# Attention and two feed-forward layers on one core: the softmax's output transposed by VectorE after a trip to DRAM

## The chip, the cores and the metric

The kernel runs on one core of one Trainium2 chip. The metric is the device time of one execution in microseconds (us).

## The reference

Three stages follow each other, all in fp32:

```python
# window attention: q, k, v are (4, 8, 576, 64)
scores = scale * np.matmul(q, k.transpose(0, 1, 3, 2))
mask = (rel >= 0) & (rel < 64)                 # rel = query position - key position
attn = np.exp(scores - max) ; attn = attn / (sum + 1e-09)
x = np.matmul(attn, v)                         # -> 2304 tokens x 512
# layer 1: w_in 512 x 2048, w_out 2048 x 512
h = x @ w_in ; r = np.maximum(h, 0.0) ; x = (r * r) @ w_out
# layer 2: the same sizes, with a rational function P(h) / Q(h) in place of r * r
return (g @ w_out).astype(np.float32)
```

## The kernel before

**Tiling.** The 2304 tokens are 18 sub-blocks of 128 (numbered 0 to 17) and five blocks: 0 to 3 of 512 tokens (four sub-blocks each), 4 of 256 (sub-blocks 16 and 17). A sub-block has two groups of 64 queries (`gl`); each sees 128 keys. Layer 1 goes through the blocks, and while block b runs, the attention of block b+1 is computed in between. So the attention of sub-blocks 8 to 11 lies in block 1, that of 12 to 15 in block 2, and that of 16 and 17 in block 3. Layer 2 follows.

**A step of a layer** is one of 16 pieces of the hidden dimension: 12 matmuls of 128x512 into `h` (L619; three products each stand for one fp32 product, split into a high and a low part), `mid1` (ScalarE takes relu and squares, VectorE subtracts for the low part, L692), and, one step later, 12 matmuls into `acc` (L638). A block of layer 1 ends with `evac1`: the result is split into `xh` and `xl` and stored to DRAM (`x2h_d`, `x2l_d`, 1 MB each).

**The attention of a sub-block** is cut into slots: `slot_q` and `slot_k` bring q and k into the layout with the head dimension on partitions; `slot_s` multiplies them (scores, L525); `softmax` masks (VectorE, L542), takes the exponential (ScalarE, L547) and multiplies by the reciprocal sum (VectorE, L551, L552 and L555); two `slot_p`, one for each group, transpose the result p, four TensorE transposes of 128x128 each (L568), and evict them from PSUM (L573, ScalarE or VectorE); `slot_x` multiplies with v (L585). From a block's second sub-block on, `slot_sx` puts the product with v of one sub-block right behind the scores of the next.

**Squares.** From sub-block 12 (`NPE`) on, q and k are not transposed by TensorE: a transfer within DRAM (`squares`) puts their 32x32 squares at the places where they belong after a transpose, the load takes them from there, and VectorE transposes within each square (L463, L485).

**Weights of layer 2** are converted during blocks 1 to 3 (`convert`): a load of the raw fp64 words (`raw`), work on ScalarE (L399, L418) and VectorE (L401 to L419), two stores (`w2h_d`, `w2l_d`).

**What sets the order.** A planner (`Plan`) takes each piece of work with a fixed cost per engine, buffers that it reads and writes, and a due time, and lists the pieces in the order in which they would start. Each engine then works in this order. All DMAs are issued by SyncE's queue (SP) in the planner's order too, and a DMA that waits holds back those behind it. To the planner all DMAs are one engine with size/360 ns each and 2 us until the data is there.

```python
KTP, QTP, SM, PT = ring("kT", 2), ring("qT", 2), ring("sm", 2), ring("pT", 2)
plan.add({"pe": 430}, tr, [src], [ps], due)                                  # slot_p
plan.add({"pe": 2150 if x_of else 900}, mm, [qt, kt] + values[0], ps + values[1], due)
```

Of the kernel before, what the change touches and what calls it, by code (L numbers as in the profile page):

```python
# [9 lines left out]
F32 = mybir.dt.float32  # L10
F32R = mybir.dt.float32r
U32 = mybir.dt.uint32
ACTF = mybir.ActivationFunctionType
ALU = mybir.AluOpType
# [122 lines left out]
def dve(n, fast=False, ptr=0):  # L137
    return 68 + 1.042 * n / (2 if fast else 1) + 61 * ptr
# [3 lines left out]
def window_attention__moe_relu2__moe_rational_kernel(  # L142
# [30 lines left out]
    NSUB = NT // 128  # L173
    blocks = [(t0, min(512, NT - t0)) for t0 in range(0, NT, 512)]
    NB = len(blocks)
    orders = (list(range(NB)), list(range(NB - 2)) + [NB - 1, NB - 2])
    NS0 = blocks[0][1] // 128
    NPE = sum(n for _, n in blocks[:3]) // 128
    scale = 1.0 / float(D) ** 0.5

    ctx.enter_context(tc.manual_schedule())
    sb = ctx.enter_context(tc.tile_pool(name="sb", bufs=1))
    dram = ctx.enter_context(tc.tile_pool(name="dram", bufs=1, space=bass.MemoryType.DRAM))
    psum = ctx.enter_context(tc.tile_pool(name="psum", bufs=1, space=bass.MemoryType.PSUM))

    V, A, P, T = nc.vector, nc.scalar, nc.gpsimd, nc.tensor
    plan = Plan()
# [6 lines left out]
    SMALL = [("cb", 2), ("coef", 6), ("na", 4), ("b1", 1)] + [(f"{x}{i}", 4) for x in ("nm", "su", "rs") for i in range(4)]  # L194
    TAGS = ([("ident", [128, 128], F32), ("mask", [128, 2, 128], F32)] +
            [(f"kT{i}", [128, HP, W + 128], F32) for i in range(2)] + [(x, [128, n], F32) for x, n in SMALL] +
            [("pad", [128, 224], F32)] +
            [(f"wi{x}{j}", [128, DM], F32R) for j in range(NF) for x in "hl"] +
            [(f"wo{j}", [128, KT, 2, 2, 128], F32R) for j in range(NF // 2)] +
            [(f"x{x}{i}", [128, 4, KT, 128], F32R) for i in range(2) for x in "hl"] +  # L200
# [10 lines left out]
    mask = sb.tile([128, 2, 128], F32, tag="mask", name="mask")  # L211
# [19 lines left out]

    sq_d = {x: dram.tile([128, HP, (NSUB - NPE) * 4, 32], F32, name=f"{x}_squares_d") for x in "kq"}


    turn = {}

    def buf(place, shape, dtype=F32, pool=sb, view=None):

        if not isinstance(place, str):
            n = turn.get(place, 0)  # L240
            turn[place] = n + 1
            place = place[n % len(place)]

        def make():
            t = pool.tile(shape, dtype, tag=place, name=place)
            return view(t) if view else t

        return Buf(plan, place, make)

    def ring(name, n):  # L250
        return tuple(f"{name}{i}" for i in range(n))
# [3 lines left out]

    ALL_PS = ("t0", "h0", "t1", "h1", "acc0", "acc1", "acc2", "acc3")
    LD, RAW, CV = ring("ld", 6), ring("raw", 3), (0, 1, 2)
    KTP, QTP, SM, PT = ring("kT", 2), ring("qT", 2), ring("sm", 2), ring("pT", 2)
    shared = {}

    def part(place, tag, shape, dtype, view, gen=0):
# [48 lines left out]
    def due_h(l, bi, j):  # L310
        return start[l, bi] + span[l, bi] * j / NF
# [4 lines left out]
    def load(dst, pieces, size, slow=1, reads=(), due=None):  # L316
        def emit(_):
            for o, i in pieces():
                nc.sync.dma_start(out=o, in_=i)
        return plan.add({"dma": size / 360 * slow}, emit, reads, [dst], due)  # L320
# [9 lines left out]
    def nat_buf(x, i):  # L330
        if i < NS0:
            return early(NF - 1 - i, x, D)
        return buf(LD, [128, H, D])
# [3 lines left out]
    def squares(nm, c, last, token):  # L337


        src = {"k": k, "q": q}[nm]  # L340
        pieces = list(toks(NPE * 128, NT - NPE * 128))
        b = sq_b[nm, c, last] = Buf(plan, f"{nm}_squares{c}{last}", None)
# [10 lines left out]
    def load_qk(i):  # L353
        for x, (nm, src) in enumerate((("k", k), ("q", q))):
            t = nat_buf(x, i)
            if i >= NPE:
                b0 = (i - NPE) * 4
                load(t, lambda t=t, nm=nm: [(
# [95 lines left out]
    def ps_buf():  # L454
        return buf(ps_places[0], [128, 512], F32, psum, cols(128))

    qT, kT, sm, pT = {}, {}, {}, {}

    def slot_q(i, due):
        src = nat["q", i]  # L460
        if i >= NPE:
            t = qT[i] = buf(QTP, [128, HP, 128])
# [15 lines left out]
    def slot_k(i, due):  # L478
        src = nat["k", i]
        if i >= NPE:  # L480
            t = kT[i] = buf(KTP, [128, HP, W + 128])
# [52 lines left out]
    def softmax(i, gl, ps):  # L534
        t = early(NF - 5 - i, gl, 128) if i < NS0 else buf(SM, [128, 4, 128])
        sm[i, gl] = t
        kind = int((2 * i + gl) % GPB == 0)
        nm, su, rs = (buf(ring(x, 4), [128, 4]) for x in ("nm", "su", "rs"))

        def top(_):  # L540
            for c in range(4):
                V.tensor_tensor_reduce(out=t.t[:, c, :], in0=ps.t[:, c, :], in1=mask[:, kind, :], scale=-scale,  # L542
                                       scalar=-NEG, op0=ALU.add, op1=ALU.min, accum_out=nm.t[:, c:c + 1])

        def exp(_):
            for c in range(4):
                A.activation(out=t.t[:, c, :], in_=t.t[:, c, :], func=ACTF.Exp, scale=-1.0, bias=nm.t[:, c:c + 1],  # L547
                             accum_out=su.t[:, c:c + 1])

        def norm(_):  # L550
            V.tensor_scalar(out=rs.t, in0=su.t, scalar1=1e-9, scalar2=None, op0=ALU.add)  # L551
            V.reciprocal(out=rs.t, in_=rs.t)  # L552

        def mul(e):
            (P if e == "pool" else V).tensor_tensor(out=t.t, in0=t.t, in1=rs.t.unsqueeze(2).to_broadcast([128, 4, 128]),  # L555
                                                    op=ALU.mult)

        plan.add({"dve": 850}, top, [ps], [t, nm])
        plan.add({"act": 1550}, exp, [nm, t], [t, su])
        plan.add({"dve": 350}, norm, [su], [rs])  # L560
        plan.add({"pool": 1400} if i < NS0 else {"dve": 690}, mul, [rs, t], [t])

    def slot_p(i, n, due):
        src, ps = sm[i, n], ps_buf()

        def tr(_):
            for c in range(4):
                T.transpose(ps.t[:, c, :], src.t[:, c, :], ident)  # L568

        plan.add({"pe": 430}, tr, [src], [ps], due)  # L570
        t = pT[i, n] = early(NF - 5 - i, 2 + n, 128) if i < NS0 else buf(PT, [128, 4, 128])
        plan.add({"act": act(512, True), "dve": dve(512)}, lambda e: (
            A.copy(out=t.t, in_=ps.t) if e == "act" else V.tensor_copy(t.t, ps.t)), [ps], [t])  # L573

    def slot_x(i, due, ps=None):
        joined = ps is not None
        ps = ps or ps_buf()
        vg = [nat["v", 2 * i + gl] for gl in range(2)]
        pt = [pT[i, n] for n in range(2)]

        def mm(_):
            for hp in range(HP):
                for gl in range(2):
                    for e in range(2):
                        T.matmul(  # L585
                            out=ps.t[e * 64:(e + 1) * 64, hp, gl * W:(gl + 1) * W],
                            lhsT=vg[gl].t[:, 2 * hp + e, :],
                            rhs=pt[gl].t[:, hp, (e ^ gl) * 64:((e ^ gl) + 1) * 64],
                            start=True, stop=True,
                        )  # L590

        if joined:
            return vg + pt, [ps], mm
        plan.add({"pe": 1250}, mm, vg + pt, [ps], due)
        split_x(i, ps)
# [208 lines left out]
    for l in range(2):  # L804
# [4 lines left out]
        for s in range(len(steps) + 1):  # L809
            lag = LAGS[l][0] if s < len(steps) - NF else LAGS[l][1]  # L810
            if s < len(steps):
                bi, j = steps[s]
                due = due_h(l, bi, j)
                if l == 0 and j == 0 and bi + 1 < NB:
                    f = blocks[bi + 1][0] // 128
# [12 lines left out]
                hp = h_mm(l, bi, j, due)  # L828
                gs[s] = (mid1 if l == 0 else mid2)(bi, j, hp)
                if l == 0 and NF - 2 <= s < NF - 2 + 4 * HP:  # L830
                    z, c = divmod(s - NF + 2, 2 * HP)
# [11 lines left out]
            if l == 0 and s < len(steps):  # L843
                while slots and slots[0][1] < due_h(0, bi, j + 1):
                    x, d = slots.pop(0)
# [43 lines left out]
```

## Time and profile before

| | us |
|---|---|
| median of 3 runs | 887.34 (884.33 to 888.93) |
| the profiled execution | 890.21 |
| its span, first to last instruction | 888.4 |
| TensorE busy | 870.5 (98%) |
| VectorE busy | 674.3 (76%) |
| ScalarE busy | 561.0 (63%) |
| mean granted TensorE clock | 0.996 |

The span starts with the first instruction; 1.8 us of the execution lie around it. TensorE's matmuls are pipelined and overlap in the records, so the price of one is read from the start of one to the start of the next, not from its length. The granted clock is a share of the full 2.4 GHz; its other level is 0.5. In the rows, PE is TensorE, DVE VectorE, ACT ScalarE, SPq SyncE's queue.

### The profile page before, as it was taken

Reading aid. Unit: us, or ns where it says so; the run is one execution under the profiler, and the core shown is the slowest. Engines: PE = TensorE matmul, PEld = TensorE weight load, DVE = VectorE, ACT = ScalarE, POOL = GpSimd, SP = SyncE. Lnnn points to the kernel's source line nnn. Section 1 sums busy time; section 2 is a strip of 40 time slices with the busy share of each in tenths; the row PEclk is TensorE's granted clock in tenths of the full one; section 3 lists DMA queues with packets and bytes.
Section 4 is the critical chain, followed back from the end, with each engine's and each line's share of the span. In section 5 each row is a group of like instructions: output and inputs, shape, how many; then the busy total and the mean of one; then the engine's idle time right before and its main releaser. Section 6 shows DMA issues by size and latency. Waiting matters only on the chain.

```text
span 888.4 us, 14088 instructions
## 1 busy us (share of the span) xinstructions
PE 870.5 (98%) x5152; PEld 726.5 (82%) x5152; DVE 674.3 (76%) x1435; ACT 561.0 (63%) x1172; POOL 11.5 (1%) x25
## 2 busy tenths in 40 slices
PE   7799999999999999999999999999999999999998
PEld 6678788888878888888899888888888888988886
DVE  6999995666466676754421899999999999999994
ACT  6778774656456554535444766676667667888764
POOL 4000000000000000000000000000000000000000
PEclk9999999999999999999999999999999999999999
DMA  9686662688855453633189910210011002100001
GB/s 230 187 243 199 188 192 84 200 219 220 223 179 184 147 184 141 238 134 126 49 313 372 361 45 0 96 48 1 1 47 48 1 1 94 49 1 24 1 1 48
DMA packets 152998, 113.64 MB, mean 128 GB/s; under 512 B 92769, under 2 KB 131681, under 8 KB 150881
## 3 DMA queue, kind: packets, MB, share of 16 engines
q1 hardware_dynamic: 152928, 112.75, 41.0%
q8 instruction: 40, 0.66, 0.3%
q14 instruction: 30, 0.24, 0.1%
HBM read 81.79 MB, written 34.08 MB: 130 GB/s over the span
## 4 chain that ended last, share of the span: by engine, by line
PE 88%; DVE 6%; DMA 3%; ACT 2%; issue 1%; SPq 0%; POOLq 0%; POOL 0%; ACTq 0%; DVEq 0%
PE h L619 30%; PE acc L640 22%; PE acc L638 19%; PE t L619 11%; PE t L525 1%; DMA raw<-in_moe_w_out_dram 1%; PE t L568 1%; DVE cvr L404 1%; PE h L585 1%; DVE cvr L407 1%; DVE sm L542 1%; DVE g L692 1%; DMA ld<-in_q_dram 0%; PE t L585 0%; DMA raw<-in_moe_w_in_dram 0%
## 5 line engine op out<-in xcount | busy, mean ns | idle before, releaser
L638 PE MATMUL acc<-g,wo 128*128 128x512 f32 (+1 forms) x960 | 215.9, 372 | 0.8 <-DVE g L692 0.8
L638 PEld LDWEIGHTS acc<-g,wo 128*128 128x128 f32 x960 | 167.3, 189 | 31.5 <-DVE g L692 1.4
L619 PE MATMUL h<-xh,wih 128*128 128x512 f32 (+1 forms) x480 | 181.1, 377 | 2.0 <-DVE rs L551 2.0
L619 PE MATMUL h<-xl,wih 128*128 128x512 f32 (+1 forms) x480 | 178.0, 371 | 0.3 <-DVE xl L603 0.3
L619 PE MATMUL h<-xh,wil 128*128 128x512 f32 (+1 forms) x480 | 178.3, 371 | 0.0
L619 PEld LDWEIGHTS h<-xh,wih 128*128 128x128 f32 x480 | 91.0, 190 | 18.0 <-ACT sm L547 2.1
L692 DVE TENSOR_TENSOR g<-cvr,g 128x512 fp32r<-128x512 f32 (+1 forms) x80 | 50.8, 635 | 71.7 <-ACT cvr L690 71.4
L619 PEld LDWEIGHTS h<-xh,wil 128*128 128x128 f32 x480 | 91.1, 190 | 16.0 <-DVE wil L419 0.4
L619 PEld LDWEIGHTS h<-xl,wih 128*128 128x128 f32 x480 | 91.1, 190 | 14.9 <-DVE xl L603 0.6
L685 ACT ACTIVATE cvr<-h 128x512 f32<-128x512 f32 (+1 forms) x80 | 44.3, 554 | 84.9 <-PE h L619 83.0
L640 PE MATMUL acc<-wo,cvr 128*128 128x512 f32 x384 | 93.1, 390 | 0.0
L640 PE MATMUL acc<-wo,g 128*128 128x512 f32 x384 | 93.1, 389 | 0.0
L640 PEld LDWEIGHTS acc<-wo,g 128*128 128x128 f32 x384 | 71.6, 188 | 14.6
L640 PEld LDWEIGHTS acc<-wo,cvr 128*128 128x128 f32 x384 | 71.5, 188 | 14.4
L736 DVE SCALAR_TENSOR_TENSOR kT<-kT,b,sm 128x512 f32<-128x512 f32 (+1 forms) x80 | 55.8, 698 | 16.4 <-ACT kT L731 13.8
L399 ACT ACTIVATE cvr<-raw 128x512 f32<-128x512 f32 x64 | 42.9, 671 | 30.3 <-DMA raw<-in_moe_w_out_dram 13.7
L738 ACT ACTIVATE raw<-kT,cb 128x512 f32<-128x512 f32 (+1 forms) x80 | 54.9, 686 | 8.8 <-DVE kT L736 6.6
L619 PE MATMUL t<-xl,wih 128*128 128x512 f32 (+1 forms) x160 | 58.9, 368 | 0.0
L619 PE MATMUL t<-xh,wil 128*128 128x512 f32 (+1 forms) x160 | 58.8, 368 | 0.0
L619 PE MATMUL t<-xh,wih 128*128 128x512 f32 (+1 forms) x160 | 58.8, 367 | 0.0
L749 DVE SCALAR_TENSOR_TENSOR pT<-pT,coef,raw 128x512 f32<-128x512 f32 (+1 forms) x80 | 55.8, 697 | 1.7
L740 ACT ACTIVATE raw<-raw,cb 128x512 f32<-128x512 f32 (+1 forms) x80 | 54.5, 681 | 1.7
(150 smaller groups left out, 1322.6 us busy)
## 6 DMA issues: line engine op xcount, KB each, us to landing
raw<-in_moe_w_in_dram SPq DMA_DIRECT2D x64, 256.0 KB, 3.4
raw<-in_moe_w_out_dram SPq DMA_DIRECT2D x32, 512.0 KB, 4.5
w2h_d<-raw SPq DMA_DIRECT2D x32, 256.0 KB, 2.1
w2l_d<-cvr SPq DMA_DIRECT2D x32, 256.0 KB, 2.1
ld<-in_v_dram SPq DMA_DIRECT2D x25, 256.0 KB, 3.9
out_dram<-ld SPq DMA_DIRECT2D x18, 256.0 KB, 2.1
x2h_d<-xh SPq DMA_DIRECT2D x4, 1024.0 KB, 5.1
x2l_d<-xl SPq DMA_DIRECT2D x4, 1024.0 KB, 7.7
```

Of the source, the lines that this page charges most:

```text
L399: plan.add({"act": act(DM)}, lambda e: A.activation(out=t.t, in_=raw.t.bitcast(F32)[:, :, 1], func=ACTF.Copy, scale=2.0 ** -112), [raw], [t])
L404: plan.add({"dve": dve(DM)}, lambda e: V.scalar_tensor_tensor(out=u(t), in0=u(t), scalar=3, in1=raw.t[:, :, 1], op0=ALU.logical_shift_left ...
L407: plan.add({"dve": dve(DM)}, lambda e: V.scalar_tensor_tensor(out=u(t), in0=raw.t[:, :, 0], scalar=29, in1=u(t), op0=ALU.logical_shift_rig ...
L619: T.matmul(out=v4(hp.t, n), lhsT=w.t[:, (c ^ 2) * 128:((c ^ 2) + 1) * 128], rhs=x.t[:, :n // 128, c, :], start=(c == 0 and z == 0), stop=( ...
L638: T.matmul(out=v4(acc[l, bi, m].t, n), lhsT=w.t[:, m, :], rhs=y.t[:, :n // 128, :], start=st, stop=en)
L640: T.matmul(out=v4(acc[l, bi, m].t, DM), lhsT=y.t[:, m, :], rhs=w.t, start=st, stop=en)
L685: plan.add({"act": act(n, True)}, lambda e: A.activation(out=r.t[:, :n], in_=hp.t[:, :n], func=ACTF.Relu), [hp], [r])
L692: plan.add({"dve": dve(n)}, lambda e: V.tensor_tensor(out=gl.t[:, :nq], in0=v4(r.t, n), in1=gh.t[:, :nq].bitcast(F32), op=ALU.subtract), [ ...
L736: plan.add({"dve": dve(n, ptr=1)}, lambda e: V.scalar_tensor_tensor(out=f(h2), in0=f(h2), scalar=b1, in1=f(ab), op0=ALU.mult, op1=ALU.add) ...
L738: plan.add({"act": act(n, ptr=1)}, lambda e: A.activation(out=f(y), in_=f(h2), func=ACTF.Ln, scale=2.0 ** -63, bias=cb[:, 0:1]), [h2], [y])
L740: plan.add({"act": act(n, ptr=1)}, lambda e: A.activation(out=f(y), in_=f(y), func=ACTF.Exp, scale=-1.0, bias=cb[:, 1:2]), [y], [y])
L749: plan.add({"dve": dve(n, ptr=1)}, lambda e: V.scalar_tensor_tensor(out=f(u), in0=f(u), scalar=coef[:, 0:1], in1=f(y), op0=ALU.subtract, o ...
```

## The change

From sub-block 8 (`NPD`) on, p takes the way of the squares. The three softmax operations write their tile with the 32-key pieces outermost, then the heads, so that each 32x32 square is complete in itself. After the multiplication the tile is stored to a DRAM tile (256 KB, one DMA), and four DMAs of 64 KB load it into the same tile with the squares rearranged: 32 queries go to 32 partitions' places and the four pieces of keys to the four groups of partitions. `slot_p` is then one VectorE instruction, a transpose within the squares of a 128x512 tile, instead of four TensorE transposes and an eviction. The product with v reads its 64 columns as two runs of 32. The ring `sm` has three tiles instead of two.

```diff
+    NPD = sum(n for _, n in blocks[:2]) // 128
...
+    p_d = dram.tile([NSUB - NPD, 2, 128, 4, 128], F32, name="p_d")
...
-    KTP, QTP, SM, PT = ring("kT", 2), ring("qT", 2), ring("sm", 2), ring("pT", 2)
+    KTP, QTP, SM, PT = ring("kT", 2), ring("qT", 2), ring("sm", 3), ring("pT", 2)
...
+        if i >= NPD:
+            keys = lambda x: x.rearrange("p (k j) -> p k j", j=32)
+            head = lambda c: t.t.rearrange("p k (h j) -> p k h j", j=32)[:, :, c, :]
+            full = lambda: t.t.rearrange("p k (h j) -> p k h j", j=32)
+            sums = lambda: rs.t.unsqueeze(1).unsqueeze(3).to_broadcast([128, 4, 4, 32])
...
-                A.activation(out=t.t[:, c, :], in_=t.t[:, c, :], func=ACTF.Exp, scale=-1.0, bias=nm.t[:, c:c + 1],
+                A.activation(out=head(c), in_=head(c), func=ACTF.Exp, scale=-1.0, bias=nm.t[:, c:c + 1],
...
+        if i >= NPD:
+            d = p_d[i - NPD, gl]
+            b = Buf(plan, f"p_d{i}{gl}", None)
+            load(b, lambda: [(d, t.t)], 1 << 18, reads=[t])
+            load(t, lambda: [(t.t[z * 32:(z + 1) * 32], d[:, z, :].rearrange("(a j) f -> j a f", j=32))
+                             for z in range(4)], 1 << 18, reads=[b])
 
     def slot_p(i, n, due):
-        src, ps = sm[i, n], ps_buf()
+        src = sm[i, n]
+        if i >= NPD:
+            t = pT[i, n] = buf(PT, [128, 4, 128])
+            plan.add({"dve": dve(512)}, lambda e: V.transpose(
+                t.t.rearrange("p a f -> p (a f)"), src.t.rearrange("p a f -> p (a f)")), [src], [t], due)
+            return
+        ps = ps_buf()
...
-                            rhs=pt[gl].t[:, hp, (e ^ gl) * 64:((e ^ gl) + 1) * 64],
+                            rhs=(pt[gl].t[:, (e ^ gl) * 2:(e ^ gl) * 2 + 2, hp * 32:(hp + 1) * 32] if i >= NPD else
+                                 pt[gl].t[:, hp, (e ^ gl) * 64:((e ^ gl) + 1) * 64]),
```

Since the planner lists everything anew, other work moves as well. Two places matter below. The first is SP's queue at the start of block 2, around the stores of block 1's result (`x2h_d`, `x2l_d`). Before:

```order
L319 DMA w2h_d<-raw_2872 128x512
L319 DMA w2l_d<-cvr 128x512
L319 DMA x2h_d<-xh_932 128x2048
L319 DMA x2l_d<-xl_972 128x2048
L319 DMA raw_3076<-in_moe_w_in_dram 128x2x256 x2
```

and with the change, where `sm_2933` and `sm_2944` are the two groups of sub-block 12:

```order
L323 DMA ld_2995<-in_v_dram 128x8x64
L323 DMA p_d<-sm_2933 128x512
L323 DMA ld_3021<-in_v_dram 128x8x64
L323 DMA p_d<-sm_2944 128x512
L323 DMA sm_2933<-p_d 32x4x128 x4
L323 DMA x2h_d<-xh_934 128x2048
L323 DMA sm_2944<-p_d 32x4x128 x4
L323 DMA x2l_d<-xl_974 128x2048
```

The loads of the first group now stand behind the store of the second, and the loads of the second behind the 1 MB store of `xh`. The start of block 1 (sub-block 8) has the same pattern, with the two loads of one raw weight between the second group's store and `x2h_d`. From the store of `xh` of block 0 to that of block 1 SP's list grows from 109 to 149 DMAs.

The second is VectorE at the same place. Before, from the multiplication of sub-block 12's second group on:

```order
L555 TENSOR_TENSOR sm_2953<-sm_2953,rs_3027 128x512
L407 SCALAR_TENSOR_TENSOR cvr<-raw_2909,cvr 128x512
L692 TENSOR_TENSOR g<-cvr,g 128x4x128
L419 TENSOR_TENSOR cvr<-cvr,raw_2909 128x512
L692 TENSOR_TENSOR g<-cvr,g 128x4x128
L401 TENSOR_SCALAR raw_3076<-raw_3076 128x512
```

and with the change (L569 is the multiplication, L718 the subtraction that was L692, L586 the new transpose):

```order
L569 TENSOR_TENSOR sm_2944<-sm_2944,rs_3012 128x512
L717 TENSOR_TENSOR cvr<-cvr 128x512
L733 TENSOR_TENSOR xl_974<-acc_1984,xh_934 128x4x128
L718 TENSOR_TENSOR g<-cvr,g 128x4x128
L405 TENSOR_SCALAR raw_2898<-raw_2898 128x512
L487 COPY kT_3051<-kT_2695 128x4x64
L408 SCALAR_TENSOR_TENSOR cvr<-cvr,raw_2898 128x512
L411 SCALAR_TENSOR_TENSOR cvr<-raw_2898,cvr 128x512
L586 STREAM_TRANSPOSE pT_3066<-sm_2933 128x512
L717 TENSOR_TENSOR cvr<-cvr 128x512
L423 TENSOR_TENSOR cvr<-cvr,raw_2898 128x512
L718 TENSOR_TENSOR g<-cvr,g 128x4x128
```

A transpose that waits for its loads now stands ahead of a subtraction on whose result the matmuls into `acc` wait. On TensorE the slots of p disappear from sub-block 8 on; the products with v of sub-blocks 8 and 12 (each joined to the scores of the next) stand nine and three matmuls later than before, the others at the same place or within a few matmuls.

## Rows read from the trace of the kernel before

**Rows 1.** The chain that ended last, by engine (part 4 of the page).

```profile
PE 88%; DVE 6%; DMA 3%; ACT 2%; issue 1%; SPq 0%; POOLq 0%; POOL 0%; ACTq 0%; DVEq 0%
```

**Rows 2.** By stage: stretch, length, busy of PE, PEld, DVE, ACT, POOL, clock, DMA share, GB/s.

```profile
148.00:245.00 97.00, 96.93 (x640) 79.23 (x639) 58.30 (x147) 54.68 (x126) 0.00 (x0) 1.00 0.80 216
245.00:345.00 100.00, 97.90 (x654) 79.62 (x653) 65.54 (x176) 56.52 (x139) 0.00 (x0) 0.98 0.54 176
345.00:440.00 95.00, 95.00 (x534) 78.03 (x533) 55.22 (x122) 47.01 (x101) 0.00 (x0) 1.00 0.39 136
```

**Rows 3.** Groups by line and shape: busy us, mean ns of one, idle before.

```profile
L568 PE MATMUL t<-ident,sm 128*128 128x128 f32 x112 | 16.8, 272 | 2.1 <-DVE sm L555 2.1
...
L573 ACT COPY pT<-t 128x512 f32<-128x512 f32 x23 | 13.4, 585 | 15.8 <-PE t L568 15.6
...
L485 DVE STREAM_TRANSPOSE kT<-ld 128x512 f32<-128x512 f32 x6 | 4.2, 705 | 2.4 <-DMA ld<-k_squares_d 2.4
```

**Rows 4.** TensorE's timeline around one slot of p: start us, length us.

```profile
266.05 0.60 PE L568 MATMUL t<-ident,sm 128*128 128x128 f32 x4
266.40 0.48 PE L619 MATMUL h<-xh,wih 128*128 128x512 f32 x1
266.72 0.40 PE L619 MATMUL h<-xl,wih 128*128 128x512 f32 x1
266.95 0.40 PE L619 MATMUL h<-xh,wil 128*128 128x512 f32 x1
```

**Rows 5.** Timelines of VectorE and TensorE: a subtraction and the matmuls that read it.

```profile
224.96 0.69 DVE L692 TENSOR_TENSOR g<-cvr,g 128x512 fp32r<-128x512 f32 x1 [1.14 <-ACT cvr L690]
...
228.34 0.95 PE L638 MATMUL acc<-g,wo 128*128 128x512 f32 x3
```

**Rows 6.** TensorE's timeline at the start of block 2, with idle time and its releaser.

```profile
253.27 0.39 PE L619 MATMUL h<-xh,wil 128*128 128x512 f32 x1
255.76 0.63 PE L568 MATMUL t<-ident,sm 128*128 128x128 f32 x4 [2.10 <-DVE sm L555]
256.14 0.48 PE L619 MATMUL h<-xh,wih 128*128 128x512 f32 x1
...
261.95 0.40 PE L619 MATMUL h<-xh,wih 128*128 128x512 f32 x1
```

**Rows 7.** By stage, as in rows 2, for the stretch behind that idle time.

```profile
256.40:260.00 3.60, 3.60 (x10) 2.82 (x10) 3.57 (x8) 3.42 (x6) 0.00 (x0) 0.53 0.51 214
```

**Rows 8.** Timelines: sub-block 8's second multiplication and product; sub-block 12's scores, multiplication, product.

```profile
150.06 0.69 DVE L555 TENSOR_TENSOR sm<-sm,rs 128x512 f32<-128x512 f32 x1
...
163.01 1.15 PE L585 MATMUL h<-pT,ld 128*64 128x64 f32 x32
...
245.52 1.10 PE L525 MATMUL t<-kT,qT 64*64 64x128 f32 x32
...
258.20 0.68 DVE L555 TENSOR_TENSOR sm<-sm,rs 128x512 f32<-128x512 f32 x1
...
269.70 0.98 PE L585 MATMUL h<-pT,ld 128*64 128x64 f32 x26
```

**Rows 9.** DMA issues: count, KB each, median us from issue to landing.

```profile
w2h_d<-raw SPq DMA_DIRECT2D x32, 256.0 KB, 2.1
...
x2h_d<-xh SPq DMA_DIRECT2D x4, 1024.0 KB, 5.1
...
ld<-q_squares_d SPq DMA_DIRECT2D x6, 256.0 KB, 3.2
...
k_squares_d<-in_k_dram SPq DMA_DIRECT2D x16, 72.0 KB, 3.6
```

**Rows 10.** SP's timeline in block 1: start us, length us of the issues (x count).

```profile
148.05 2.54 SPq L319 DMA_DIRECT2D k_squares_d<-in_k_dram  x4
...
206.34 0.34 SPq L319 DMA_DIRECT2D w2h_d<-raw  x1
...
241.34 2.51 SPq L319 DMA_DIRECT2D raw<-in_moe_w_out_dram  x1
```

More of the change, by code (lines that the diff above doesn't have):

```diff
@@ L196, in window_attention__moe_relu2__moe_rational_kernel @@
             [(f"kT{i}", [128, HP, W + 128], F32) for i in range(2)] + [(x, [128, n], F32) for x, n in SMALL] +
-            [("pad", [128, 224], F32)] +
+            [("pad", [128, 208], F32)] + [("sm2", [128, 4, 128], F32)] +
             [(f"wi{x}{j}", [128, DM], F32R) for j in range(NF) for x in "hl"] +
@@ L538, in softmax @@
         nm, su, rs = (buf(ring(x, 4), [128, 4]) for x in ("nm", "su", "rs"))
+        if i >= NPD:
[3 more added lines that the diff above has]
+            sums = lambda: rs.t.unsqueeze(1).unsqueeze(3).to_broadcast([128, 4, 4, 32])
+        else:
+            keys = lambda x: x
+            head = lambda c: t.t[:, c, :]
+            full = lambda: t.t
+            sums = lambda: rs.t.unsqueeze(2).to_broadcast([128, 4, 128])
         def top(_):
             for c in range(4):
-                V.tensor_tensor_reduce(out=t.t[:, c, :], in0=ps.t[:, c, :], in1=mask[:, kind, :], scale=-scale,
+                V.tensor_tensor_reduce(out=head(c), in0=keys(ps.t[:, c, :]), in1=keys(mask[:, kind, :]), scale=-scale,
                                        scalar=-NEG, op0=ALU.add, op1=ALU.min, accum_out=nm.t[:, c:c + 1])
@@ L554, in mul @@
         def mul(e):
-            (P if e == "pool" else V).tensor_tensor(out=t.t, in0=t.t, in1=rs.t.unsqueeze(2).to_broadcast([128, 4, 128]),
-                                                    op=ALU.mult)
+            (P if e == "pool" else V).tensor_tensor(out=full(), in0=full(), in1=sums(), op=ALU.mult)
         plan.add({"dve": 850}, top, [ps], [t, nm])
```

## The prediction

> **What bounds the kernel now.** I read the chain of waits first: 88% of it is TensorE [rows 1]. Then the table by stage, cut where block 1, 2 and 3 of layer 1 run, because the change touches only these: TensorE is busy 96.9 of 97 us, 97.9 of 100 and 95.0 of 95, VectorE 58, 66 and 55 us, ScalarE 55, 57 and 47 us [rows 2]. So in these stages only two things move the end: time that TensorE no longer spends, and time for which it newly waits. The one gap in 292 us is in the second stage, and it is looked at below [rows 6].
>
> **What is removed.** Twenty slots (sub-blocks 8 to 17, two groups each) lose four TensorE transposes. The mean of one transpose, 272 ns [rows 3], is the length of a pipelined instruction and is no price; the price is read from starts. A slot starts at 266.05 and the next matmul at 266.40, which is 0.35 us; that matmul takes 0.32 us to the next start where the one after takes 0.23, so changing over costs another 0.09 [rows 4]. 0.44 us a slot, all on the path since TensorE has no idle time there: 20 x 0.44 = **8.8 us**. With the slots go their evictions from PSUM, 15 or so by ScalarE at 585 ns [rows 3] and the rest by VectorE: neither engine is the bound, so nothing is counted.
>
> **A stall that goes.** At the start of block 2 TensorE starts a matmul at 253.27 and its next work, the transposes of sub-block 12, only at 255.76, because the multiplication of the softmax (VectorE, L555) was late: 2.49 less 0.23, so 2.26 us idle. After this the granted clock is 0.53 on average from 256.4 to 260.0, so mostly at the lower of its two levels, 1.2 GHz [rows 7], and the 18 matmuls from 256.14 to 261.95 take 5.81 us where 18 x 0.23 = 4.1 is usual [rows 4, 6]. Idle and slow clock together cost 2.26 + 1.7 = **3.9 us**. The instruction that waited no longer exists, so this place is free. What is late next there is the group that reads p, the product with v.
>
> **What is added on VectorE and ScalarE.** Twenty 32x32-square transposes of 128x512 at 705 ns, the row of the same instruction on k [rows 3]: 14 us over 292 us in which VectorE idles 113 us [rows 2]. The score, exponential and multiplication steps keep their counts and sizes and only write in runs of 32; I take nothing for that, at most some per cent of engines that are half idle. The cost is not their length but their place: VectorE works in its order, and behind each transpose stands the subtraction (L692) that the second matmul of a step needs. Its cover: the subtraction that starts at 224.96 ends at 225.65 and its reader starts at 228.34 [rows 5], so 2.7 us.
>
> **What is added on the way of p.** Per group one store of 256 KB and four loads of 64 KB, on SP's queue, between the multiplication and the transpose. The trace of before has no such load, so it is bounded by neighbours. Issue: 0.34 us for a store of 256 KB, 2.54/4 = 0.64 for one of the transfers that make k's squares [rows 10]. Landing: 2.1 us for a store of 256 KB, 3.2 for the 256 KB load of squares in 512-byte runs, 3.6 for 72 KB in 128-byte runs [rows 9]. So a round trip is 0.34 + 2.1 + 3 x (0.34 to 0.64) + (2.1 to 3.6) + 0.71 for the transpose = 6.2 to 8.7 us, if SP is not busy with others. I take 8, since the four loads resemble the squares most.
>
> The room for it is least where a block begins, because a 1 MB store of x2h stands on SP among the new transfers. In sub-block 8 the second multiplication ends at 150.06 + 0.69 = 150.75 and the product with v starts at 163.01 [rows 8], 12.3 us; without the slot between them and with the nine matmuls by which the product moves back in the new order it is 12.3 - 0.4 + 2.1 = 14.0. In it SP issues four loads, a store, two weight loads, x2h's store and four loads: 12 x (0.34 to 0.64), then 2.1 (a store alone) to 5.1 us of landing (x2h's, which is ahead [rows 9]) and 0.71 = 6.9 to 13.5 us. It just fits. In the sub-blocks inside a block no such store is in the way and the 8 us fit easily.
>
> **The place where it may not fit** is sub-block 12, at the start of block 2. Scores start at 245.52, the second multiplication ends at 258.9, 13.4 us later, and the product starts at 269.70 [rows 8]. In the new order the product stands three matmuls later; the room from the scores is 24.2 - 3.9 (the stall) - 0.9 (two slots) + 0.7 = 20.1 us. On SP, a store, four loads, x2h's store and four loads follow the end of the multiplication: 10 x (0.34 to 0.64) of issues, 2.1 to 5.1 us of landing and 0.71 = 6.2 to 12.2 us. So p is ready 19.6 to 25.6 us after the scores and TensorE waits 0 to 5.5 us; the multiplication may also come up to 2 us earlier, now that no wait of TensorE (2.26 us) lies ahead of it. I take 2, a little under the middle, and as an idle time of 2.26 us was followed by the lower clock, its 1.7 us too [rows 6, 7]: **+3.7 us**.
>
> **SP's queue in block 1.** From 148.05 to its load at 241.34 SP issues 115 DMAs whose lengths sum to 78 us [rows 10], of 97. Eight groups more add 8 x (0.34 + 4 x (0.34 to 0.64)) = 14 to 23 us, and the stage gets some 4 us shorter: 92 to 101 of 93. The squares of q and k have no hurry before block 2, and some DMAs drain after 241, so I count the lower half: **+1.5 us** of late weights or p, between 0 and 8.
>
> **The sum.** -8.8 - 3.9 + 3.7 + 1.5 = -7.5 us. The profiled execution took 890.2 us (888.4 span and 1.8 around it) and would take 882.7; the median of the runs shown is 887.34, 2.9 lower, so I forecast 887.3 - 7.5 = **879.8 us**.
>
> **A rule against it.** The rows say that a transpose on TensorE costs 0.44 us of the path and one on VectorE none of it [rows 2, 4]. The Trainium skill, VectorE: DVE Perf Modes, section Rules for kernel authors, advises TensorE for a transpose of 128x128 if PSUM may be its destination, as it may here. By the rule the old form is the better one and the removed 8.8 us would not be a gain; the rows of this kernel decide, because its bound is TensorE.
>
> **Rivals.**
> 1. *All of it hides.* Sub-block 12 is not late and SP keeps up: -8.8 - 3.9 = -12.7, 874.6 us. For it: 19.6 us at sub-block 12 is less than its room. Against it: SP's sum.
> 2. *SP becomes the bound of block 1.* At the upper end of the sums, 101 of 93 us, SP runs 8 us late. The loads of weights and of p come late and TensorE waits, 5 us in all after what drains behind 241, with the lower clock twice (3.4): -8.8 - 3.9 + 3.7 + 8.4 = -0.6, 886.7 us, no change that can be told (the runs of this kernel tell about 0.5%, 4.4 us). For it: 0.64 us an issue, and DMA engines 80% busy in this stage [rows 2]. Against it: in block 2 the DMA share falls to 0.54, so what comes late can still drain.
> 3. *The four loads of a group land one after another instead of side by side.* This ends slower. With 3.6 us each [rows 9] the round trip is 0.34 + 2.1 + 14.4 + 0.71 = 17.6 us, 3.6 more than the 14.0 us of room, which I take for each of the eight sub-blocks of blocks 1 and 2. Each wait is over 2.26 us and so brings the slow clock: 8 x (3.6 + 1.7) = 42.4, less 12.7: +29.7, 917 us. It decides from a round trip of 14.0 us on. Against it: a load that gathers the same 512-byte runs lands in 3.2 us [rows 9]. The Trainium skill, VectorE: DVE Perf Modes, section The three transpose paths, warns that a plain DMA with access-pattern strides for a transpose is 19 times slower than its hardware path when the innermost destination stride is large; by that rule this rival would hold. The row of 3.2 us speaks against it, as each run here is contiguous.
>
> **How the numbers follow.** Forecast 0.50, rival 1 0.15, rival 2 0.25, rival 3 0.10. Forecast and rival 1 are faster by over 0.5% (below 882.9): 0.65; rival 2 is within: 0.25; rival 3 slower: 0.10. The range takes rival 1 at the bottom with 1 us for the runs' own spread, and rival 2 at the top with the same: 873.6 to 887.7; outside are rival 3 and the tails, about 2 in 10.
>
> **What would show it.** Right: TensorE's transposes of sm gone after sub-block 7; 0.44 us less from start to start at each; the idle time at sub-block 12 now ahead of the product with v, at most 5 us; SP issuing almost without a break in block 1. Wrong: the product with v, or the second matmul of a step, waiting in several sub-blocks, with granted clock near 0.5 behind each wait; VectorE idle ahead of its new transposes for over 2.7 us; a landing of the four loads far above 3.6 us.

## The result and the profile after

The changed kernel takes **893.14 us** (median of 6 runs, 890.46 to 894.32) against 887.32 for the kernel before (6 runs, 884.33 to 888.93). The ratio is **1.0065**, with a 95% interval from 1.0042 to 1.0088: slower by about 5.8 us, where 879.8 us, faster, had been forecast. The time lies above the range of 873.6 to 887.7 us.

In the changed kernel the line numbers are some 26 higher: L645 is the matmul into `h`, L664 the one into `acc`, L718 the subtraction, L586 the new transpose on VectorE, L403 and L405 the first steps of a weight's conversion, L323 every DMA. The windows by stage, with the columns of [rows 2]:

```profile
148.00:245.00 97.00, 88.91 (x571) 71.79 (x570) 57.52 (x149) 49.42 (x124) 0.00 (x0) 0.95 0.78 210
245.00:345.00 100.00, 97.78 (x642) 79.11 (x641) 71.46 (x187) 54.21 (x135) 0.00 (x0) 1.00 0.81 246
345.00:440.00 95.00, 95.00 (x527) 78.09 (x526) 59.19 (x128) 49.64 (x105) 0.00 (x0) 1.00 0.53 179
```

The loss lies in one stage, block 1 (148 to 245 us): TensorE idles 8.1 us there, where it idled 0.1 [rows 2], and the mean granted clock is 0.95 instead of 1.00. The two later stages are as good as before. So the question is what happens in block 1. The waits of the whole run (engine, tile and line, what was waited for, us in total, times, longest):

```profile
ACT cvr L403 <- DMA raw<-in_moe_w_out_dram: 23.6, 14, 5.2
...
ACT cvr L403 <- DMA raw<-in_moe_w_in_dram: 18.5, 12, 3.5
DVE pT L586 <- DMA sm<-p_d: 17.1, 13, 2.2
...
PE acc L664 <- DVE g L718: 7.9, 4, 4.7
...
PE h L645 <- DVE xl L629: 3.6, 3, 2.1
```

No wait of TensorE for a new transpose is among them (at the product with v, L610, there is one wait of 0.7 us for an old eviction, which the kernel before has too). What TensorE waits for most is the subtraction, and VectorE and ScalarE ahead of it wait for two kinds of data from DMAs: the raw weights of layer 2 (42.1 us in all; 26.3 in the kernel before) and the rearranged p. Both are issued by SP. Its timeline, in the stretch with the longest stall (start us, length us of the issues):

```profile
219.52 2.96 SPq L323 DMA_DIRECT2D k_squares_d<-in_k_dram  x4
222.52 0.62 SPq L323 DMA_DIRECT2D raw<-in_moe_w_out_dram  x1
223.24 0.38 SPq L323 DMA_DIRECT2D w2h_d<-raw  x1
224.09 0.32 SPq L323 DMA_DIRECT2D p_d<-sm  x1
224.47 0.49 SPq L323 DMA_DIRECT2D w2l_d<-cvr  x1
225.30 0.35 SPq L323 DMA_DIRECT2D p_d<-sm  x1
225.70 0.90 SPq L323 DMA_DIRECT2D ld<-in_v_dram  x1
229.10 4.64 SPq L323 DMA_DIRECT2D sm<-p_d  x8
```

The raw weights are issued at 222.52, behind four transfers of squares that take 2.96 us of the queue. The loads of p stand behind a wait for the store of p to land: from 226.60 to 229.10 SP issues nothing. Then eight issues take 4.64 us. The timelines of ScalarE, VectorE and TensorE show what this does, in that order:

```profile
227.82 0.66 ACT L403 ACTIVATE cvr<-raw 128x512 f32<-128x512 f32 x1 [4.52 <-DMA raw<-in_moe_w_out_dram]
...
233.49 0.71 DVE L586 STREAM_TRANSPOSE pT<-sm 128x512 f32<-128x512 f32 x1 [1.95 <-DMA sm<-p_d]
235.74 0.71 DVE L586 STREAM_TRANSPOSE pT<-sm 128x512 f32<-128x512 f32 x1 [1.53 <-DMA sm<-p_d]
236.37 0.65 DVE L718 TENSOR_TENSOR g<-cvr,g 128x512 fp32r<-128x512 f32 x1
...
232.00 0.39 PE L664 MATMUL acc<-g,wo 128*128 128x512 f32 x1
237.07 3.35 PE L664 MATMUL acc<-g,wo 128*128 128x512 f32 x7 [4.69 <-DVE g L718]
```

ScalarE stands still 4.52 us for the weights; in its order the relu and the squares of the next step come behind. VectorE gets to the two transposes late, waits 1.95 and 1.53 us for p, and only then does the subtraction that TensorE has been waiting for; what ends last here are the loads of p. That is 4.69 us of idle TensorE. A second place, at 190 to 198 us, has weights alone: the raw load is issued at 185.57, ScalarE waits 5.16 us for it, and TensorE loses 2.12 us to `xl` (L629) and 1.28 us to a load of q issued at 193.07. Behind both the granted clock is near 0.5 (windows):

```profile
198.30:201.70 3.40, 3.40 (x11) 2.76 (x10) 2.77 (x7) 2.67 (x10) 0.00 (x0) 0.55 0.80 181
235.90:242.70 6.80, 5.62 (x14) 4.32 (x14) 3.27 (x6) 2.53 (x4) 0.00 (x0) 0.53 0.98 240
```

At a clock of 0.55 and 0.53 the 3.40 and 5.62 busy us are worth 1.9 and 3.0 us of full clock, so 1.5 + 2.6 = 4.1 us go there. With 8.1 us idle that is 12.2 us. The rest of the timeline bears this out. The two profiled executions do not reach block 1 at the same time: a matmul of block 0 that is the same in both kernels starts at 131.42 us before and at 133.70 with the change, ahead of every trip of p. These 2.3 us are no cost of the change that any run shows; the executions of the kernel before lie up to 6 us apart. The rows, before and after:

```profile
131.42 2.88 PE L638 MATMUL acc<-g,wo 128*128 128x512 f32 x12
```

```profile
133.70 2.88 PE L664 MATMUL acc<-g,wo 128*128 128x512 f32 x12
```

Counted from there, the product with v of sub-block 11 starts after 109.2 us (at 242.90) instead of 100.6 (at 231.98), 8.6 us later, and eight slots (8 x 0.44 = 3.5 us) should have brought it earlier: 12.1 us lost, which the idle time and the slow clock account for.

The landings (count, KB each, median us from issue to landing) do not stand out for p: 3.2 and 2.5 us. Those of the weights' stores rose from 2.1 [rows 9]:

```profile
w2h_d<-raw SPq DMA_DIRECT2D x32, 256.0 KB, 3.1
...
p_d<-sm SPq DMA_DIRECT2D x20, 256.0 KB, 3.2
sm<-p_d SPq DMA_DIRECT2D x80, 64.0 KB, 2.5
```

From the trace alone four theories stand:
- **A**: SP's queue issues too many DMAs in block 1, and what hurries stands behind what doesn't.
- **B**: the 16 DMA engines carry too much (10.5 MB more in all).
- **C**: the planner's new order, or the moved buffers, cost it, whatever the DMAs do.
- **D**: the trip of p is too long in itself for the place in which its transpose stands in VectorE's order.

### The profile page after: what moved, and what is told of

The parts are those of the page before. It is cut to its first block, busy times and chain, and to the rows that moved or that the text cites. A ratio compares the mean times of both kernels' runs of the same rounds, so it can differ in the third digit from the quotient of the medians.

```text
span 892.5 us, 14099 instructions
## 1 busy us (share of the span) xinstructions
PE 865.2 (97%) x5072; PEld 721.6 (81%) x5072; DVE 681.3 (76%) x1448; ACT 554.4 (62%) x1159; POOL 11.5 (1%) x25
## 2 busy tenths in 40 slices
DMA packets 167397, 124.14 MB, mean 139 GB/s; under 512 B 94368, under 2 KB 143520, under 8 KB 165280
## 4 chain that ended last, share of the span: by engine, by line
PE 86%; DVE 7%; DMA 4%; issue 1%; ACT 1%; SPq 0%; POOLq 0%; POOL 0%; DVEq 0%; ACTq 0%
PE h L645 29%; PE acc L666 22%; PE acc L664 19%; PE t L645 11%; DMA raw<-in_moe_w_in_dram 2%; PE t L529 2%; DVE cvr L411 1%; DVE cvr L408 1%; PE h L610 1%; DMA ld<-q_squares_d 1%; DVE raw L405 1%; DVE g L718 1%; DMA p_d<-sm 1%; DVE sm L556 1%; DMA ld<-in_q_dram 1%
## 5 line engine op out<-in xcount | busy, mean ns | idle before, releaser
L664 PE MATMUL acc<-g,wo 128*128 128x512 f32 (+1 forms) x960 | 218.1, 374 | 9.2 <-DVE g L718 7.9
L664 PEld LDWEIGHTS acc<-g,wo 128*128 128x128 f32 x960 | 168.5, 190 | 41.6 <-DVE g L718 10.0
L645 PE MATMUL h<-xh,wih 128*128 128x512 f32 (+1 forms) x480 | 179.9, 375 | 4.5 <-DVE xl L629 3.3
L645 PE MATMUL h<-xl,wih 128*128 128x512 f32 (+1 forms) x480 | 177.4, 370 | 0.3 <-DVE xl L629 0.3
L645 PE MATMUL h<-xh,wil 128*128 128x512 f32 (+1 forms) x480 | 177.3, 369 | 0.0
L645 PEld LDWEIGHTS h<-xh,wih 128*128 128x128 f32 x480 | 91.1, 190 | 21.3 <-DVE xl L629 4.2
L718 DVE TENSOR_TENSOR g<-cvr,g 128x512 fp32r<-128x512 f32 (+1 forms) x80 | 50.7, 634 | 71.4 <-ACT cvr L716 71.3
L645 PEld LDWEIGHTS h<-xh,wil 128*128 128x128 f32 x480 | 90.8, 189 | 15.5
L645 PEld LDWEIGHTS h<-xl,wih 128*128 128x128 f32 x480 | 90.9, 189 | 15.2 <-DVE xl L629 0.6
L403 ACT ACTIVATE cvr<-raw 128x512 f32<-128x512 f32 x64 | 42.6, 668 | 47.4 <-DMA raw<-in_moe_w_out_dram 23.6
L645 PE MATMUL t<-xl,wih 128*128 128x512 f32 (+1 forms) x160 | 58.9, 368 | 0.0
L645 PE MATMUL t<-xh,wil 128*128 128x512 f32 (+1 forms) x160 | 58.8, 368 | 0.0
L645 PE MATMUL t<-xh,wih 128*128 128x512 f32 (+1 forms) x160 | 58.8, 367 | 0.0
```

What stands on the lines that cost most here:

```text
L403: plan.add({"act": act(DM)}, lambda e: A.activation(out=t.t, in_=raw.t.bitcast(F32)[:, :, 1], func=ACTF.Copy, scale=2.0 ** -112), [raw], [t])
L645: T.matmul(out=v4(hp.t, n), lhsT=w.t[:, (c ^ 2) * 128:((c ^ 2) + 1) * 128], rhs=x.t[:, :n // 128, c, :], start=(c == 0 and z == 0), stop=( ...
L664: T.matmul(out=v4(acc[l, bi, m].t, n), lhsT=w.t[:, m, :], rhs=y.t[:, :n // 128, :], start=st, stop=en)
L718: plan.add({"dve": dve(n)}, lambda e: V.tensor_tensor(out=gl.t[:, :nq], in0=v4(r.t, n), in1=gh.t[:, :nq].bitcast(F32), op=ALU.subtract), [ ...
```

## The experiments

Every time is given with its ratio to the kernel before, measured beside it, and the 95% interval. Differences in us are the difference of the ratios times 887.3. Diffs are against the changed kernel unless said otherwise.

**1. The same order without the trip.** The store and the four loads keep their places in the plan but move nothing; p's round trip is left out.

```diff
-            load(b, lambda: [(d, t.t)], 1 << 18, reads=[t])
-            load(t, lambda: [(t.t[z * 32:(z + 1) * 32], d[:, z, :].rearrange("(a j) f -> j a f", j=32))
-                             for z in range(4)], 1 << 18, reads=[b])
+            load(b, lambda: [], 1 << 18, reads=[t])
+            load(t, lambda: [], 1 << 18, reads=[b])
```

> The changed kernel without the store and the loads of p (80 + 20 DMAs less; the transposes read the tile as the multiplication left it, so p is computed in a wrong arrangement), planner's order unchanged. Theory A (SP's queue issues too much in block 1, so weights and p come late): 876 to 880 us, the 8.8 us of the slots plus what of the old 3.9 us stall goes; idle time of TensorE in block 1 under 3 us. Theory B (the DMA engines carry too much): the same, 876 to 880. Theory C (the planner's new order, or the moved buffers, cost the time by themselves): 888 to 893, the idle time at VectorE's subtraction stays.

Measured: 876.44 us, ratio 0.9882 [0.9864, 0.9899], so 10.5 us below the kernel before. TensorE is busy 97.00 of 97 and 100.00 of 100 us in blocks 1 and 2. The twenty slots are worth what was forecast or a little more, the new order costs nothing that can be seen, and C falls. The 16.2 us between this run and the change (1.0065 - 0.9882 = 1.83%) are the trip's.

**2. The trip on GpSimd's queue.** `q` is a new argument of `load` that names the issuing engine; `P` is GpSimd.

```diff
-            load(b, lambda: [(d, t.t)], 1 << 18, reads=[t])
+            load(b, lambda: [(d, t.t)], 1 << 18, reads=[t], q=P)
-                             for z in range(4)], 1 << 18, reads=[b])
+                             for z in range(4)], 1 << 18, reads=[b], q=P)
```

> All DMAs of p issued by GpSimd's queue, which has nothing else to do after 35 us, instead of SP's. Same bytes, same engines, same order. Theory A: SP issues in block 1 as before the change, TensorE no longer waits for late weights there: 877 to 883 us. Theory B: nothing changes, 890 to 894. Theory D (the round trip itself is too long for VectorE's order, whoever issues it): 888 to 893, with the waits of the new transposes still ahead of the subtraction.

Measured: 912.43 us, 1.0295 [1.0273, 1.0316], slower than any theory had expected. The waits for raw weights fall to 9.8 and 7.4 us in all, as A wants, but every transpose now waits: store and loads land 4.0 us after issue (3.2 and 2.5 on SP's queue), and GpSimd, too, holds the loads until the store has landed. The waits, as above:

```profile
DVE pT L586 <- DMA sm<-p_d: 61.8, 20, 8.9
POOL sm L323 <- DMA p_d<-sm: 52.6, 15, 7.6
```

So a trip that is long enough does what D says. Whether it is D or A at the length it has on SP is left open by this run, as it lengthens one while it relieves the other.

**3 and 4. Where the loss lies.** The trip from sub-block 12 on alone (`NPD = sum(n for _, n in blocks[:3]) // 128`), and the trip in sub-blocks 8 to 11 alone (the four tests `i >= NPD` become `NPD <= i < NPE`).

> The change from sub-block 12 on only: block 1 is as before, blocks 2 and 3 with the trip. Theory A: SP is busy for 31 us of 100 in block 2 before the change, so it has room: 12 slots x 0.44 = 5.3 us and up to 3.9 for the old stall, 878 to 883 us. Theory B: DMA share in block 2 is 0.54 before, so the same, 878 to 883. Theory D: half of the loss remains, 886 to 890.

> The other half: the change for sub-blocks 8 to 11 only, those of block 1. Theories A and B: all of the loss is here, without the gain of the other twelve slots: 893 to 898 us, idle time of TensorE in block 1 of 9 us or more. Theory D: half of the loss, 888 to 892.

Measured: 885.85 us, 0.9987 [0.9971, 1.0003], from 12 on, between the ranges expected; 895.0 us, 1.009 [1.0067, 1.0114], with 8 to 11 alone, as A and B expected. The eight trips of block 1 make a loss by themselves, 8.0 us. From 12 on, block 1 is at 97.00 of 97, but block 2 at 94.44 of 100, with 47 us of waits for raw weights in the whole run. Twelve slots should bring 5.3 us and 1.2 were seen; why this plan is worse in block 2 than the change's own was not followed further.

**5. The trip goes elsewhere.** Store and loads stand as in the change and issue as often, but the loads write a second DRAM tensor, `p_e`, so nothing waits for them. The transposes take the squares unrearranged (the rearrangement is left out).

```diff
-            load(t, lambda: [(t.t[z * 32:(z + 1) * 32], d[:, z, :].rearrange("(a j) f -> j a f", j=32))
+            load(t, lambda: [(p_e[i - NPD, gl][z * 32:(z + 1) * 32], d[:, z, :].rearrange("(a j) f -> j a f", j=32))
                              for z in range(4)], 1 << 18, reads=[b])
```

> Stores and loads of p are issued as in the change, in the same places of the queue and with the same bytes, but the four loads write a second DRAM tensor, so no transpose waits for them (the transposed p is then of the unrearranged squares: p's rearrangement is left out). Theories A (SP's queue issues too much in block 1) and B (the DMA engines carry too much): the loss stays, 888 to 893 us, TensorE busy 89 to 91 of the 97 us of 148 to 245. Theory D (the trip's own length holds VectorE in its order): the loss goes but for the weights that land late, 876 to 880 us, TensorE 95 to 97 of 97.

Measured: 903.7 us, 1.0167 [1.0147, 1.0186], slower than anything A or B had expected. No wait for p is left at all, and still the weights are later than in the change:

```profile
ACT cvr L403 <- DMA raw<-in_moe_w_in_dram: 39.5, 14, 6.7
...
ACT cvr L403 <- DMA raw<-in_moe_w_out_dram: 31.5, 15, 7.5
```

Without D's wait the loss stays and grows by 9.0 us. A likely reason for the growth can be read on SP: from 148 to 345 us one such load takes 0.69 us of SP (mean of 56) where a load into SBUF took 0.55 (mean of 64), so the issues alone take 56 x 0.14 = 8 us more. As the run adds this of itself, it speaks against D as the main cause but does not rule out a part of D; run 7 tests that.

**6. SP relieved, the trip untouched.** The transfers that put q's and k's squares in place are issued by GpSimd.

```diff
-        load(b, parts, S * 512, 2, reads=[token])
+        load(b, parts, S * 512, 2, reads=[token], q=P)
```

> The change, with the DMAs that rearrange q and k (72 KB each, in block 1) issued by GpSimd instead of SP: SP issues about 80 instead of 155 in block 1. Theory A: the weights and the loads of p come on time, 878 to 884 us, ScalarE's waits for raw weights back to about 26 us in all, no wait of 4 us behind the store of p. Theory D: 886 to 891 us, the waits of VectorE for p stay at about 17 us.

Measured: **879.55 us, 0.9899 [0.9881, 0.9918]**, 9.0 us below the kernel before and the best of all complete kernels here. Block 1 is full again (windows, as above):

```profile
148.00:245.00 97.00, 96.63 (x652) 78.80 (x651) 65.09 (x167) 54.32 (x130) 6.90 (x10) 1.00 0.76 232
245.00:345.00 100.00, 98.91 (x649) 80.34 (x648) 73.54 (x196) 54.21 (x136) 0.00 (x0) 1.00 0.76 231
```

SP's own waits from 160 to 245 us tell what was missing in the change. There all its waits sum to 9.7 us, and the issues take 73.6 of the 85 us, so the queue had under 2 us of free time. Here the issues take 44.2 us and SP waits for work that is not ready yet:

```profile
SPq L323 <- PE h L610: 11.3, 3, 6.1
SPq L323 <- DMA w2h_d<-raw: 9.9, 4, 4.3
SPq L323 <- DVE sm L569: 9.1, 6, 3.1
```

VectorE's waits for p halve on their own (8.8 us, from 17.1), and ScalarE's for raw weights fall from 42.1 to 30.2 us (26.3 in the kernel before). The Trainium skill, Perfetto Trace Analysis, section DMA Optimizations, advises to spread DMAs over the engines that can issue them where the issuing engine, and not the transfer, is what is busy; this run agrees, with 14.7 us (0.9899 against 1.0065). By itself it does not tell A from B, because from GpSimd the same squares also load the DMA engines less: in the kernel before the DMA share of block 1 falls from 0.80 to 0.64 with this edit (run 9). Runs 10 and 11 tell them apart.

**7 and 8. The transposes placed later.** The planner counts 3.5 us more for the way of p (an item on an engine of its own for each group), so that the transposes stand later in VectorE's order; SP has the same DMAs to issue. Run 8 has both this and the edit of run 6.

```diff
-    ENGINES = ("pe", "act", "dve", "pool", "dma")
+    ENGINES = ("pe", "act", "dve", "pool", "dma", "way0", "way1")
...
+            plan.add({f"way{gl}": 3500}, lambda e: None, [t], [t])
```

> The change, with 3.5 us added to what the planner believes a trip takes, so that each new transpose stands later in VectorE's order; SP's queue issues the same. Theory D: VectorE's waits for p fall from 17 to under 5 us, and 882 to 888 us. Theory A: the weights stay late, 889 to 893 us; if the products with v are placed too soon behind, a wait there takes the place of it, 890 to 896.

> Both edits at once: squares of q and k issued by GpSimd and the transposes placed 3.5 us later. If A and D are each a part of the loss: 877 to 882 us, below the kernel before by about 0.8%, TensorE 95 to 97 of 97 in block 1. If B (the DMA engines' load of 10.5 MB more) is the cause: 888 to 893 us.

Measured: 896.51 us, 1.0082 [1.006, 1.0104], alone, just above what A had for products placed too soon; 882.14 us, 0.9922 [0.9902, 0.9941], with the squares on GpSimd. Alone, VectorE's waits for p fall to 1.1 us, but the weights are as late as in the change (29.4 and 15.7 us), some products with v now wait for the transpose (2.9 and 1.7 us in all), and nothing is won. So D is no part of the loss that this edit can bring back. Run 8 is not below run 6, so with SP relieved the later place wins nothing either.

**9. Control: the kernel before with the squares on GpSimd** (the edit of run 6).

> Control: the kernel before with the same DMAs of the squares of q and k issued by GpSimd. If SP's queue costs the kernel before nothing worth speaking of, 884 to 888 us, and the change is worth 0.6 to 1.0% on top of it; if the squares on SP already cost it, 876 to 882 us, and the gain of the run with the squares on GpSimd was not the change's.

Measured: 885.99 us, 0.999 [0.9974, 1.0007]. SP's load cost the kernel before nothing that can be told. So the gain of run 6 is the change's own: 8.1 us against this run (0.9899 against 0.999).

**10 and 11. Issues or bytes.** Run 10 loads p back with one plain DMA, `load(t, lambda: [(t.t, d)], ...)`: all bytes, three issues fewer for each group (the rearrangement is left out). Run 11 keeps all five issues and moves a quarter of the bytes (the first of the four squares of each row; the rest of the trip, and the rearrangement, are left out).

> The change with one plain load of 256 KB where four rearranged loads of 64 KB stood: the same bytes, three issues less for each half (the rearrangement of the squares is left out). Theory A (issues): 877 to 882 us, block 1 at 96 to 97 of 97. Theory B (bytes on the DMA engines): 888 to 893 us.

> The change with its five issues for each half, where each carries a quarter of the bytes (the first of four squares of each row; the rest of p's round trip is left out). Theory A (issues): 887 to 893 us, the weights as late as in the change. Theory B (bytes): 876 to 881 us.

Measured: 880.53 us, 0.9929 [0.9904, 0.9954], with few issues; 888.03 us, 1.000 [0.9986, 1.0014], with few bytes. The windows of block 1, run 10 first:

```profile
148.00:245.00 97.00, 94.32 (x631) 76.29 (x630) 60.08 (x149) 50.95 (x119) 0.00 (x0) 0.98 0.88 243
```

```profile
148.00:245.00 97.00, 90.85 (x583) 73.32 (x582) 56.84 (x144) 49.53 (x118) 0.00 (x0) 0.96 0.72 189
```

The DMA engines carry 243 GB/s at a share of 0.88 where the time is good, and 189 at 0.72 where it is bad; the change has 210 at 0.78. So it is not the DMA engines' capacity that runs out, and B falls. Taking issues away wins 12.1 us of the 16.2 (1.0065 - 0.9929 = 1.36%), though block 1 stays at 94.32 of 97 where 96 to 97 had been expected. Taking bytes away wins 5.8, so the five issues are not all of the loss. Both runs also take packets away, about as many (158757 and 159718 in all, from 167397), so packets do not explain the 6.3 us between them; of the 5.8 us, the share of the bytes and that of the packets are not separated. In run 11 p's store lands in 2.3 us instead of 3.2 and VectorE waits 9.6 us for p instead of 17.1.

**12. Half the dose.** Only q's squares go to GpSimd (`q=P if nm == "q" else nc.sync`).

> Half of the dose: only q's squares are issued by GpSimd, k's stay on SP (some 30 issues less in block 1, 112 against 142; the kernel before has 118). Theory A: between the change and the run with both moved, and near it if only what is over the kernel before's number costs: 879 to 885 us. Theory B: 888 to 893 us.

Measured: 883.79 us, 0.9955 [0.9935, 0.9975], between the change and run 6, as A has it. (Counted as in the table below, SP issues 121 DMAs here, 139 in the change and 114 in the kernel before.)

**All runs on one scale.** The profiled executions reach block 1 up to 5 us apart, so each is counted from the matmul of block 0 named above, over the 97 us from 16.6 to 113.6 us behind it (148.02 to 245.02 in the kernel before). Given are the DMAs that SP issues, the sum of their lengths in its timeline, how many raw weight loads are among them (the two halves of a piece of w_in counted apart), and when the sixth of these is issued, in us behind the matmul; beside it the time against the kernel before.

| kernel | issues | their us | raw loads | sixth raw load | us |
|---|---|---|---|---|---|
| 1, no trip | 112 | 78.2 | 18 | 46.0 | -10.5 |
| 6, squares on GpSimd | 97 | 51.7 | 18 | 47.2 | -9.0 |
| 8, both edits | 97 | 55.1 | 18 | 46.1 | -6.9 |
| 10, one plain load | 125 | 81.1 | 18 | 48.7 | -6.3 |
| 12, q's squares on GpSimd | 121 | 69.8 | 18 | 49.4 | -4.0 |
| 3, trip from 12 on | 114 | 78.4 | 18 | 44.4 | -1.2 |
| 9, before, squares on GpSimd | 58 | 31.1 | 18 | 41.9 | -0.9 |
| before | 114 | 77.7 | 18 | 44.4 | 0 |
| 11, few bytes | 140 | 84.1 | 15 | 51.9 | 0.0 |
| the change | 139 | 83.6 | 15 | 51.9 | +5.8 |
| 7, transposes later | 139 | 88.3 | 15 | 49.6 | +7.3 |
| 4, trip in 8 to 11 | 137 | 85.0 | 15 | 52.4 | +8.0 |
| 5, trip elsewhere | 130 | 87.6 | 14 | 55.0 | +14.8 |
| 2, trip on GpSimd | 102 | 74.6 | 16 | 48.5 | +26.2 |

The column of raw loads tells the groups apart: with 18 of them through SP in the stage a kernel is at least as fast as the kernel before, with 15 and fewer none is faster. (Run 2 stands apart: there p is what comes late.) A part of that is the lost time itself, as a stage that runs late also asks later. The sixth raw load is free of this, because in the change TensorE's first idle time in block 1 comes behind it and ends at 195.55 us. Before, and with the change:

```profile
175.82 0.59 SPq L319 DMA_DIRECT2D raw<-in_moe_w_out_dram  x1
```

```profile
185.57 0.34 SPq L323 DMA_DIRECT2D raw<-in_moe_w_out_dram  x1
```

From the matmul that is 44.4 and 51.9 us, so SP is 7.5 us late before TensorE has waited once in block 1. The load lands 4.5 us after its issue in both: the issue is late, not the transfer. Run 11 has the change's queue in every column and is still 5.8 us faster, so the queue's lateness is the larger part of the loss and not the whole.

## Why the prediction was wrong, step by step

- **Removed, 8.8 us: right.** Run 1 is 10.5 us faster without the trip, interval 9.0 to 12.1, and run 6 is 9.0 us faster with the trip when SP is free.
- **A stall that goes, 3.9 us: at most half.** Run 1 leaves 10.5 - 8.8 = 1.7 us for it. Run 9 has no such stall in its profile (100.00 of 100 us in block 2) and takes the same time as the kernel before, whose profile has it. The stall was read in an execution that was 2.9 us above the median, and the forecast took it off the median; that it belongs to that execution more than to the median is argued, not shown.
- **VectorE's place, put at nothing: on the path, but not the cause.** The transposes do wait, 17.1 us in all, and the longest stall of TensorE, 4.69 us, comes by a subtraction that stands behind two of them. But run 7 removes these waits and wins nothing, and run 5 has none and loses more; in both the weights come late.
- **Sub-block 12, +3.7 us: did not occur.** The scores start at 256.43, the second transpose ends at 275.28 + 0.71 = 275.99, 19.6 us later, which was the lower end of the estimate, and the product starts at 276.44 with no wait.
- **SP's queue, +1.5 us between 0 and 8: the step that failed.** Its sum was good: 16 stores at 0.46 us and 64 loads at 0.55 (means from 148 to 345) make 2.66 us a group, 21 for eight, within the 14 to 23, and with 78 us it gives 99 of 93. What failed is what was made of it: "The squares of q and k have no hurry before block 2, and some DMAs drain after 241, so I count the lower half". In SP's order what has no hurry does not let the others pass: 56 transfers of squares were issued in block 1 as before (148 to 245 us), with weights behind them, and what was left over at the end of the stage was weights (15 raw loads got through instead of 18). Measured by run 6 against the change, this term is 14.7 us, and by run 1 the whole trip is 16.2; 12.2 can be read as idle time and slow clock in block 1. By run 11, 5.8 us hang on p's bytes or packets and not on the number of issues.
- **Rival 2** named the mechanism, SP as the bound of block 1, and priced it at 8.4 us, by 5 us of waits and the lower clock twice. The lower clock did come twice (4.1 us); the idle time was 8.1 us. It was short because it took the waits from SP's overrun at the end of the stage, while the sixth raw load was already 7.5 us late. That ScalarE and VectorE pass each late load on to the step that TensorE needs, and that SP itself waits 3.7 us in block 1 for stores of p to land with everything behind it, is read from the timelines; no run prices it.
- **Rival 1** did not come: only run 1, which has no trip, comes near its 874.6 us (876.4).
- **Rival 3** falls: the four loads land 2.5 us after issue. The 19 times of the Trainium skill, VectorE: DVE Perf Modes, section The three transpose paths, do not show in any row for these runs of 512 bytes. The prediction let this rival hang on that rule; but the Trainium skill states it for a large stride in the innermost dimension of the destination, and here each run is contiguous, so the rule does not speak of these loads.
- **The rule** of the Trainium skill, the same page, section Rules for kernel authors, that advises TensorE for such a transpose: the change as made bears it out, by 5.8 us; run 6 speaks against it for this kernel, by 9.0 us, once the queue that carries the trip has room.

What stays open: why the trip from sub-block 12 on alone has stalls in block 2 that the change does not have. That the planner's price for a DMA (its bytes, not its issue time) let it put so much on one queue is read from the code; a plan with issue times was not tried.

## What to carry to other kernels

Before an extra round trip through DRAM is put beside a full TensorE, add up the issue times on the queue that will carry it, not only bytes and landings: here 5 more issues for each group of 64 queries, 2.7 us of SP, made most of the price (run 10, with 2 issues for 5, gives back 12.1 of 16.2 us). When the sum passes the length of the stage, price it as a bound: in an ordered queue the overrun falls on whatever stands behind, urgent or not, and here idle times of 2.1 and 1.3 us close together, and one of 4.7 us, were each followed by a granted clock near 0.54. The remedy that worked is another queue for transfers that can wait (run 6). Fewer issues would be another; run 10 shows their worth, but with the rearrangement left out. The trip itself did better on the queue with the shorter landing (2.5 to 3.2 us on SP's, 4.0 on GpSimd's, run 2).

## What the runs showed of the hardware

The same transfers of squares, issued by GpSimd, make fewer packets: in run 6 the total falls while the megabytes stay (the page of the change, then that of run 6), and in the kernel before the DMA share of block 1 falls from 0.80 to 0.64 with them (run 9). That was not expected and is not explained here.

```profile
DMA packets 167397, 124.14 MB, mean 139 GB/s; under 512 B 94368, under 2 KB 143520, under 8 KB 165280
```

```profile
DMA packets 144358, 124.14 MB, mean 141 GB/s; under 512 B 69792, under 2 KB 119968, under 8 KB 142240
```

The time that an issue takes of SP depends on where the transfer goes: 0.55 us for a 64 KB load into SBUF, 0.69 for the same runs into DRAM (run 5). It hardly depends on the bytes: a load of 16 KB takes 0.53 us (run 11), a plain one of 256 KB 0.47 (run 10; all means from 148 to 345 us).
